# Two FFN weights loaded in 32-row pieces, and w3 transposed by VectorE in place of TensorE

## The chip, the cores and the metric

The kernel runs on one core of a Trainium2 chip. The metric is the device time of one execution in microseconds (us): before the change the median of three runs is 872.85 us, from 872.33 to 872.88. The core has five engines with a queue each: TensorE (PE; its weight loads are listed as PEld), VectorE (DVE), ScalarE (ACT), GpSimd (POOL) and SyncE (SP). Here SP only issues transfers between HBM and SBUF; some transfers are issued by ScalarE.

## The reference

Two blocks in a row. The first is a retention layer over 8 batches, 8 heads, 576 positions and a head size of 64; its result is laid out as 4608 tokens of 512 features. The second is a multiplicative feed-forward network on these tokens:

```python
    scores = scale * np.matmul(q, k.transpose(0, 1, 3, 2))
    ret = scores * Dmat[None, :, :, :]          # Dmat: gamma ** (i - j) for i >= j, else 0
    attn_out = np.matmul(ret, v).astype(np.float32)
    x = np.ascontiguousarray(attn_out.transpose(0, 2, 1, 3)).reshape(B * S, H * D)   # 4608 x 512
    a = x @ w1                                  # 512 x 1024
    b = x @ w2                                  # 512 x 1024
    h = a * b @ w3                              # 1024 x 1024
    return (h @ w_out).astype(np.float32)       # 1024 x 512
```

The four weights arrive as 64-bit floats, q, k and v as 32-bit floats. The output is 32-bit.

## The kernel before

**Algebra.** `(a * b) @ w3 @ w_out` is computed as `(a * b) @ (w3 @ w_out)`. The product w3o = w3 @ w_out (1024 x 512) is made once, on the chip, in what is called the w3 stage below. The products x @ w1, x @ w2 (the function `up`, L476 to L521) and (a * b) @ w3o (`down`, L583 to L638) use Strassen-like schemes with seven block products and sums of blocks on VectorE, ScalarE and GpSimd.

**Weights.** TensorE and VectorE work here on 32-bit floats, so each weight is converted on the chip. A weight is cut into blocks of 128 partitions by 512 numbers (the list `blocks`, L309 to L315): 16 blocks of w1 and w2, then 8 of w_out (one row tile of 128 rows each), then 16 of w3 (row tile `ft` of 128 rows, two halves of 512 columns). SP loads a block as pairs of 32-bit words into one of five `raw` buffers (`load_block`, L319), 512 KB a block; w3 and w_out blocks are one transfer each (L337). `begin_block` (L353) and `end_block` (L378) convert it: on VectorE L362 and L366 take out exponent and top mantissa, L369 adds the low word; on ScalarE L372 and L373 bring the exponent into place; on VectorE L383 adds the sign and L392 multiplies. That is five VectorE operations and two ScalarE operations for a block. The conversion is a generator (`conversion`, L401): it begins a block before it ends the one before it, and the rest of the kernel advances it by single steps (`convert`, L422, or up to a given block, `convert_up_to`, L428), which places its instructions between others in the engines' queues. When a block is ended, the block five further on is loaded into its buffer.

**The w3 stage.** TensorE contracts over partitions, so w3 @ w_out needs w3 with its columns on the partitions. `w3_tr` (L433) turns a row tile of w3 by eight TensorE transposes of 128x128 into two PSUM banks, which ScalarE copies to a tile `w3T` (L440). `w3_mm` (L443) multiplies its eight 128x128 pieces with the eight tiles of w_out, in two halves of four, into one bank `ps`, and ScalarE copies the result to `w3o` (L451). `w3` and `w3T` have two buffers each.

**Order.** Each engine works through its queue in the order in which the program emits it. The order around the stage is written by hand in the loop at L730: while products of `up` are left (`todo`), an `up` is emitted with steps of the conversion between its sums. Then, for each row tile, come the first half of the products of the tile before, the transposes of this tile, the second half of the products, and ten steps of conversion. A gate in `end_block` (L387) holds the conversion of w3 to two row tiles ahead of the transposes.

**After the stage.** `w3_sums` (L526) makes four sums of blocks of w3o on VectorE (L536); they are emitted one by one between the sums of the next `up` (`aside`). Then comes the first `down`, whose own sums are L565, L569 and L571. The attention inputs for the next two batches are loaded (L109) into SBUF space that the conversion's buffers had held, and scaled by GpSimd (L212). From 320 us on, k and q tiles are loaded in pieces of 32 rows (`load_blocks`, L168, issued at L179) and transposed by VectorE in 32x32 blocks (`front_blocks`, L198).

Of the kernel before, what the change touches and what calls it, by code (L numbers as in the profile page):

```python
# [8 lines left out]
F32 = mybir.dt.float32  # L9
I32 = mybir.dt.int32  # L10
U32 = mybir.dt.uint32
ALU = mybir.AluOpType
PSUM = bass.MemoryType.PSUM

# [22 lines left out]
def kernel(  # L39
# [13 lines left out]
    nc = tc.nc  # L53
    moe_w1, moe_w2, moe_w3, moe_w_out = (
        w.bitcast(I32).rearrange("r (c t) -> r c t", t=2) for w in (moe_w1, moe_w2, moe_w3, moe_w_out))
    B, H, S, D = q.shape
    DM = H * D
    DF = moe_w3.shape[0]
    CV = 512
    P = 128  # L60
    NP = H // 2
    NB2 = B // 2


    NC = (S + P - 1) // P
    short = S - (NC - 1) * P
    sizes = [short] + [P] * (NC - 1)
    starts = [0] + [short + c * P for c in range(NC - 1)]
    G = NB2 * NC
    NB = 3  # L70
    TB = S // NB
    NT = 2 * TB // P
    KD = DM // P
    KF = DF // P
# [13 lines left out]
    pools = {}  # L88
# [6 lines left out]
    open_attention(att_part)  # L95
    acc = ctx.enter_context(tc.tile_pool(name="acc", bufs=7, space=PSUM))
    st_ps = ctx.enter_context(tc.tile_pool(name="st_ps", bufs=1, space=PSUM))

    ctx.enter_context(tc.manual_schedule())

    live = {}
# [14 lines left out]
    ident = const.tile([P, P], F32, tag="ident", name="ident")  # L116
# [10 lines left out]
    gq = const.tile([P, NC, H], F32, tag="gq", name="gq")  # L127
    gqs = const.tile([P, NP, S // 32], F32, tag="gqs", name="gqs")
    dq = ffn.tile([P, 4, 2, TB], F32, tag="c", name="dq", bufs=1).rearrange("p a b s -> p (a b s)")[:H, :S]
# [6 lines left out]
    for c in (0, slice(1, NC)):  # L136
        n = short if c == 0 else P
# [16 lines left out]
    def strassen_weights(fp):  # L154
# [7 lines left out]
        tt("S4", "A12", "S2", ALU.subtract)  # L162
        live["S", fp] = True
        yield

    BL = 32

    def load_blocks(g, nm):  # L168

        i, c = divmod(g, NC)  # L170
        n = sizes[c] // BL
        t = pools["ld"].tile([P, 2 * NP, P // BL, BL], F32, tag="ld_q", name="bl_" + nm)
        src = {"k": k, "q": q}[nm][2 * i:2 * i + 2].rearrange("b (p a) s d -> a (b p) s d", a=2)
        for a in range(2):
            for f in range(D // BL):
                part = (a * (D // BL) + f) * BL
                for m in range(n):
                    s0 = starts[c] + m * BL
                    nc.sync.dma_start(t[part:part + BL, :, m, :],  # L179
                                      src[a, :, s0:s0 + BL, f * BL:(f + 1) * BL].rearrange("m r x -> r m x"))  # L180
        live["bl_" + nm, g] = t

    def scale_blocks(g):
# [3 lines left out]
        for b in range(2):  # L187
            part = t[:, b * NP:(b + 1) * NP, :n, :]
            nc.gpsimd.tensor_tensor(
                out=part, in0=part, in1=gqs[:, :, n0:n0 + n].unsqueeze(3).to_broadcast([P, NP, n, BL]),  # L190
                op=ALU.mult)

    def front_blocks(g):
        c = g % NC
        n = sizes[c] // BL
        for nm in "kq":
            dst = pools["fr"].tile([P, 2, NP, P], F32, tag=nm + "T", name=nm + "T", bufs=1 if nm == "k" else 2)
            nc.vector.transpose(  # L198
# [16 lines left out]
    def front(g, names="kq"):  # L215
        c = g % NC
        sz = sizes[c]
        for nm in names:
            src = live[nm, g]
            dst = pools["fr"].tile([P, 2, NP, P], F32, tag=nm + "T", name=nm + "T",  # L220
                                   bufs=1 if nm == "k" and g >= NC else 2)
# [87 lines left out]
    blocks = []  # L309
# [2 lines left out]
            for r in range(2):  # L312
                blocks.append((("w12", fp, j, r), w))
    blocks += [(("wo", g), moe_w_out) for g in range(KF)]
    blocks += [(("w3", ft, g0), moe_w3) for ft in range(KF) for g0 in range(0, DF, CV)]  # L315
    at = {key: n for n, (key, _) in enumerate(blocks)}
    loaded, begun, converted, turned = [0], [0], [0], [0]

    def load_block():  # L319
        n = loaded[0]  # L320
        if n == len(blocks):
            return
        key, w = blocks[n]
        t = raw.tile([P, CV, 2], I32, tag="raw", name="raw", bufs=5)
        if key[0] == "w12":
            _, fp, _, r = key
            src = w[2 * r * P:2 * (r + 1) * P, fp * QC:(fp + 1) * QC, :]
            t2 = t.rearrange("p (c n) t -> p c n t", c=2)
            if r == 0:
                nc.sync.dma_start(t2, src.rearrange("(c p) n t -> p c n t", p=P))  # L330
            else:
                for half in range(2):
                    nc.sync.dma_start(t2[heads[half]],
                                      src.rearrange("(c a d) n t -> a d c n t", a=2, d=D)[1 - half])
        else:
            r, c0 = (key[1], 0) if key[0] == "wo" else key[1:]
            nc.sync.dma_start(t, w[r * P:(r + 1) * P, c0:c0 + CV, :])  # L337
        live["raw", n] = t
        loaded[0] += 1

    def converted_to(n):
        key, _ = blocks[n]
        if key[0] == "w12":
            _, fp, j, r = key
            return wA[fp // 2][:, j, 2 * r:2 * r + 2, fp % 2 * QC:fp % 2 * QC + QC]
        if key[0] == "wo":
            return live["wo"][:, key[1], :]
        _, ft, g0 = key
        if ("w3", ft) not in live:
            live["w3", ft] = pools["wst"].tile([P, DF], F32, tag="w3", name="w3")  # L350
        return live["w3", ft][:, g0:g0 + CV]

    def begin_block():  # L353
        n = begun[0]
# [23 lines left out]
    def end_block():  # L378
        n = converted[0]
        hi = live["raw", n][:, :, 1]  # L380
        e, m = live["em", n]
        vec = nc.vector
        vec.scalar_tensor_tensor(e, in0=hi, scalar=-(1 << 31), in1=e,  # L383
                                 op0=ALU.bitwise_and, op1=ALU.bitwise_or)
        yield
        key = blocks[n][0]
        while not (key[0] == "w12" or "wo" in live and (key[0] == "wo" or key[1] < turned[0] + 2)):  # L387
            yield "wait"
        out, m, e = converted_to(n), m.bitcast(F32), e.bitcast(F32)
        if key[0] == "w12":  # L390
            m, e = (x.rearrange("p (c n) -> p c n", c=2) for x in (m, e))
        vec.scalar_tensor_tensor(out, in0=m, scalar=2.0 ** -20, in1=e, op0=ALU.mult, op1=ALU.mult)  # L392
        converted[0] += 1

        if n >= 4:
            load_block()
        if key[0] == "w12" and key[1] > 0 and key[2:] == (1, 1):
            yield from strassen_weights(key[1])
        yield
# [22 lines left out]
    def convert(n):  # L422

        for _ in range(n):
            if go_on() is not None:
                return

    def convert_up_to(n):  # L428
        while converted[0] < n:
            assert go_on() is None  # L430


    def w3_tr(ft):  # L433
        t = pools["wst"].tile([P, KF, P], F32, tag="w3T", name="w3T")
        for i in range(0, KF, NP):
            tp = acc.tile([P, NP, P], F32, tag="acc", name="tp")
            for n in range(NP):
                nc.tensor.transpose(tp[:, n, :], live["w3", ft][:, (i + n) * P:(i + n + 1) * P],  # L438
                                    ident)
            nc.scalar.copy(t[:, i:i + NP, :], tp)  # L440
        live["w3T", ft] = t

    def w3_mm(ft, part):  # L443
        if part == 0:
            live["w3ps"] = acc.tile([P, DM], F32, tag="acc", name="ps")
        ps = live["w3ps"]
        for g in range(part * NP, part * NP + NP):
            nc.tensor.matmul(ps, live["w3T", ft][:, g, :], live["wo"][:, g, :],  # L448
                             start=(g == 0), stop=(g == KF - 1))
        if part == 1:  # L450
            nc.scalar.copy(live["w3o"][:, ft, :], ps)  # L451

    every = [(i, n) for i in range(NB2) for n in range(NB)]

# [190 lines left out]


    load_block()
    load(0, "v")
    load_block()
    load(1, "kq")  # L650
    load_block()
# [65 lines left out]
    for a in range(2):  # L717
        for f in range(D // BL):
            part = (a * (D // BL) + f) * BL
# [6 lines left out]
    live["wo"] = pools["wst"].tile([P, KF, DM], F32, tag="wo", name="wo", bufs=1)  # L726
    live["w3o"] = w3op.tile([P, KF, DM], F32, tag="w3o", name="w3o")
    todo = [(0, 1, 2), (0, 0, 3), (0, 1, 3)] + [(0, 2, fp) for fp in range(NQ - 1)]
    multiplied = 0
    while multiplied < KF:  # L730
        if todo:
            first = converted[0] < 4 * NQ
            up(*todo.pop(0), conv=2 if first else 1)
            convert(0 if first else 3)
        ft = multiplied
        begun_ft = ft < turned[0]
        if begun_ft:
            w3_mm(ft, 0)
        if turned[0] < KF and (not todo or converted[0] > at["w3", turned[0], DF - CV]):
            convert_up_to(at["w3", turned[0], DF - CV] + 1)  # L740
            w3_tr(turned[0])
            turned[0] += 1
        if begun_ft:
            w3_mm(ft, 1)
            multiplied += 1
        if not todo:
            convert(10)
    w3_part.close()


# [15 lines left out]
    todo = [(down, (0, 0), (0, 1)), (down, (1, 0), (1, 1)), (down, (0, 2), (1, 2))]  # L766
# [38 lines left out]
    for g in range(NC, G):  # L805
        c = g % NC
        n = -(-len(todo) // (NC - c))
# [78 lines left out]
```

## Time and profile before

| What | Value |
|---|---|
| median of three runs | 872.85 us |
| profiled execution: its own time | 872.62 us |
| profiled execution: span, first to last instruction | 870.7 us |
| mean granted TensorE clock | 0.998 of full speed |
| TensorE busy | 851.9 us, 98% of the span |
| VectorE busy | 458.3 us, 53% |
| ScalarE busy | 194.7 us, 22% |
| GpSimd busy | 111.8 us, 13% |
| w3 stage on TensorE: 64 products of 128x512 (128 passes, L448) | 56.4 us busy |
| w3 stage on TensorE: 64 transposes (L438) | 8.5 us busy |
| blocks of w3 and w_out (L337), issue to landing, median | 3.6 us |

The profile is one execution, recorded by the hardware. Times are in microseconds, means of one instruction in nanoseconds. "L438" is a line of the kernel. A group of instructions is given as line, engine, operation, the tile written, an arrow, and the tiles read, with its shape. The chain that ended last is followed back from the last instruction to what released each step, so its shares tell on whose time the end depends. In a timeline a line gives start, length, engine, line, operation and count, and in square brackets how long the engine had been idle and what ended that. A TensorE product of 32-bit floats stands as two passes. Matmuls overlap, and their ends are modelled, so rows of busy matmuls add up to a little more than the time they cover; the distance from start to start is the better measure.

### The profile page before, as it was taken

The page shows a single profiled execution, that of the slowest core. Times are in us where ns is not written, and L with a number is a line of the kernel's source. Part 1 is how long each engine was busy: PE and PEld are TensorE (multiplying, and loading weights), DVE is VectorE, ACT ScalarE, POOL GpSimd, SP SyncE. Part 2 cuts the span into 40 slices and gives each one's busy share as a digit, 9 for nine tenths or more (in the row PEclk, how much of TensorE's full clock was granted, in tenths as well). Part 3 has the DMA queues.
Part 4 walks back from the last instruction along what each step waited for, and adds up shares of the span by engine and source line. Part 5 has one row for each costly group of instructions (what it writes and reads, how often), then busy time and mean ns, then how long its engine had stood idle before and what let it go on. Part 6 is the DMA issues. An engine that isn't in the chain of part 4 may idle for free.

```text
span 870.7 us, 15305 instructions
## 1 busy us (share of the span) xinstructions
PE 851.9 (98%) x6373; PEld 779.0 (89%) x6373; DVE 458.3 (53%) x781; ACT 194.7 (22%) x390; POOL 111.8 (13%) x91
## 2 busy tenths in 40 slices
PE   5899999999999999999999999999999999999998
PEld 5899999645888999999999999999999999999996
DVE  4799998973543344643544544534543434334343
ACT  3676333553022221101111101111101100001000
POOL 3000020002001323201212030230300101000000
PEclk9999999999999999999999999999999999999999
DMA  9993443437035444515242335061300000000001
GB/s 194 218 223 107 98 99 104 139 120 108 1 77 118 114 63 82 95 28 93 49 84 44 55 68 96 27 104 34 59 25 25 2 25 1 25 24 1 25 1 49
DMA packets 187332, 63.20 MB, mean 73 GB/s; under 512 B 175480, under 2 KB 175480, under 8 KB 187264
## 3 DMA queue, kind: packets, MB, share of 16 engines
q1 hardware_dynamic: 154624, 54.07, 29.2%
q10 hardware_dynamic: 32640, 8.16, 4.9%
q8 instruction: 50, 0.82, 0.4%
q14 instruction: 18, 0.15, 0.1%
HBM read 52.76 MB, written 9.44 MB: 71 GB/s over the span
## 4 chain that ended last, share of the span: by engine, by line
PE 88%; DVE 3%; issue 1%; DMA 1%; ACT 1%; DVEq 0%; ACTq 0%; SPq 0%
PE up L493 46%; PE po L599 25%; PE ps L448 6%; PE sc L241 4%; PE xps L298 3%; PE xps L291 2%; PE tp L226 1%; PE st L263 1%; DVE c L498 1%; PE tp L438 1%; DVE e L383 0%; DMA raw<-in_moe_w_dram 0%; ACT e L372 0%; DVE ab L519 0%; DVE w L392 0%
## 5 line engine op out<-in xcount | busy, mean ns | idle before, releaser
L498 DVE TENSOR_TENSOR c<-up,c 128x384 f32<-128x384 f32 x240 | 133.2, 555 | 198.0 <-PE up L493 193.2
L493 PE MATMUL up<-xT,wA 128*128 128x192 f32 x1152 | 213.5, 329 | 1.0 <-ACT xT L303 1.0
L493 PEld LDWEIGHTS up<-xT,wA 128*128 128x128 f32 x1152 | 191.9, 191 | 3.6 <-ACT xT L303 1.2
L493 PE MATMUL up<-T,wS 128*128 128x192 f32 x768 | 141.1, 327 | 2.1 <-DVE T L467 2.1
L493 PEld LDWEIGHTS up<-T,wS 128*128 128x128 f32 x768 | 127.8, 191 | 2.4 <-issue 2.4
L599 PE MATMUL po<-w3o,ab 128*128 128x256 f32 x456 | 104.2, 381 | 0.3 <-ACT ot L621 0.3
L599 PEld LDWEIGHTS po<-w3o,ab 128*128 128x128 f32 x456 | 86.0, 190 | 12.1 <-ACT ot L621 0.7
L603 DVE TENSOR_TENSOR ot<-po,ot 128x256 f32<-128x256 f32 x90 | 38.1, 424 | 72.3 <-PE po L599 70.6
L513 ACT COPY c<-up 128x384 f32<-128x384 f32 x48 | 22.9, 477 | 226.3 <-PE up L493 222.0
L493 PE MATMUL up<-xT,wS 128*128 128x192 f32 x384 | 70.6, 327 | 0.6 <-DVE c L498 0.5
L493 PE MATMUL up<-T,wA 128*128 128x192 f32 x384 | 70.3, 326 | 0.0
L244 DVE TENSOR_TENSOR pm<-sc,mask 128x512 f32<-128x512 f32 (+1 forms) x80 | 45.5, 628 | 46.7 <-PE sc L241 46.5
L599 PE MATMUL po<-wB,forms 128*128 128x256 f32 x288 | 65.1, 379 | 0.0
L493 PEld LDWEIGHTS up<-xT,wS 128*128 128x128 f32 x384 | 63.6, 190 | 1.5 <-DVE c L498 1.5
L493 PEld LDWEIGHTS up<-T,wA 128*128 128x128 f32 x384 | 63.7, 190 | 0.0
L599 PEld LDWEIGHTS po<-wB,forms 128*128 128x128 f32 x288 | 54.8, 190 | 7.3
L212 POOL TENSOR_TENSOR ld_v<-ld_v,gk 128x1024 f32<-128x1024 f32 (+1 forms) x17 | 32.3, 1900 | 213.6 <-DMA ld_v<-in_v_dram 186.3
L448 PE MATMUL ps<-wo,w3T 128*128 128x512 f32 x128 | 56.4, 593 | 0.2 <-ACT w3T L440 0.2
L506 ACT COPY c<-up 128x384 f32<-128x384 f32 x48 | 22.8, 476 | 117.4 <-PE up L493 68.4
L467 POOL TENSOR_TENSOR T<-xT,T 128x384 f32<-128x384 f32 x20 | 20.9, 1043 | 217.1 <-PE up L493 215.4
L519 DVE TENSOR_TENSOR ab<-c 128x768 f32<-128x768 f32 x48 | 46.6, 972 | 3.8
L448 PEld LDWEIGHTS ps<-wo,w3T 128*128 128x128 f32 x128 | 23.7, 190 | 27.2 <-issue 26.7
(75 smaller groups left out, 817.8 us busy)
## 6 DMA issues: line engine op xcount, KB each, us to landing
raw<-in_moe_w_dram SPq DMA_DIRECT2D x24, 512.0 KB, 3.7
out_dram<-ot SPq DMA_DIRECT2D x24, 256.0 KB, 2.0
bl_q<-in_q_dram SPq DMA_DIRECT2D x136, 32.0 KB, 2.1
bl_k<-in_k_dram SPq DMA_DIRECT2D x136, 32.0 KB, 2.2
raw<-in_moe_w_dram SPq DMA_DIRECT2D x16, 256.0 KB, 6.1
ld_k<-in_k_dram SPq DMA_DIRECT2D x8, 512.0 KB, 7.1
ld_q<-in_q_dram SPq DMA_DIRECT2D x8, 512.0 KB, 8.2
ld_v<-in_v_dram SPq DMA_DIRECT2D x8, 512.0 KB, 7.4
```

The lines of the kernel that those rows point to most:

```text
L212: nc.gpsimd.tensor_tensor(out=t, in0=t, in1=gam[:sz, c].unsqueeze(1).unsqueeze(3).to_broadcast([sz, 2, H, D]), op=ALU.mult)
L241: nc.tensor.matmul(sc[j][:sz, p, :sz], kT[hs, b, p, :sz], qT[hs, b, p, :sz], start=True, stop=True)
L244: nc.vector.tensor_mul(pm[:sz, b, j, :, :sz], sc[j][:sz, :, :sz], mask[:sz, :sz].unsqueeze(1).to_broadcast([sz, NP, sz]))
L298: nc.tensor.matmul(banks[r][heads[half], b, n, :sz], vs[:sz, b * H + 2 * p + j, :], pm[:sz, b, j, p, :sz], start=(c == 0 and m == 0), stop ...
L448: nc.tensor.matmul(ps, live["w3T", ft][:, g, :], live["wo"][:, g, :], start=(g == 0), stop=(g == KF - 1))
L493: nc.tensor.matmul(ps[:, w, :], a[:, w, r, :], b[:, r, :], start=(new and w == r == 0), stop=(w == r == 1), skip_group_check=True)
L498: nc.vector.tensor_add(c[:, to], ps, c[:, sb])
L506: nc.scalar.copy(c[:, 0], p1)
L513: nc.scalar.copy(c[:, 0], p1)
L519: nc.vector.tensor_mul(ab[:, 4 * fp:4 * fp + 4, :], c[:, :, 0, :], c[:, :, 1, :])
L599: nc.tensor.matmul(ps[nm], a[A][:, f, :], live["W"][B][:, f, :], start=(f == 0 and not on), stop=(f == NP - 1), skip_group_check=True)
L603: nc.vector.tensor_add(ot[:, to[0], to[1]], ps[nm], ot[:, sb[0], sb[1]])
```

## The change

Four things change together.

- **w_out's loads.** Row tile `i` no longer holds rows 128 i to 128 i + 127. It holds, for four groups `a` of 32 partitions, rows 256 a + 32 i to 256 a + 32 i + 31, and is loaded by four transfers of 32 rows.
- **w3's loads.** A block (row tile `ft`, half `h`) is loaded by four transfers into 32 partitions each. Group `a` of 32 partitions takes columns from the quarter `a` (256 columns) of w3; the four sub-blocks `j` of 32 rows of the tile stand beside one another in the free dimension, in pieces of 128 numbers (1 KB).
- **The transposes.** When the second half of a row tile is converted, one VectorE transpose of 32x32 blocks (128 x 1024) writes `w3T`. Because of the new places of rows and columns, its partitions then match those of w_out's tiles. `w3_tr`, its 64 TensorE transposes and its 16 ScalarE copies are gone. `w3` has one buffer, `w3T` three.
- **The order.** `w3_mm` makes all eight products of a row tile at once. The gate lets the conversion run three row tiles ahead of the products, and the loop takes eleven steps of conversion per row tile, the eleventh being the transpose.

The conversion itself keeps its operations; the last one of a w3 block writes four runs of 128 numbers.

```diff
@@ -58,6 +60,8 @@
+    BL = 32
+    QP = P // BL
...
@@ -312,9 +314,9 @@
             for r in range(2):
                 blocks.append((("w12", fp, j, r), w))
     blocks += [(("wo", g), moe_w_out) for g in range(KF)]
-    blocks += [(("w3", ft, g0), moe_w3) for ft in range(KF) for g0 in range(0, DF, CV)]
+    blocks += [(("w3", ft, h), moe_w3) for ft in range(KF) for h in range(DF // CV)]
     at = {key: n for n, (key, _) in enumerate(blocks)}
-    loaded, begun, converted, turned = [0], [0], [0], [0]
+    loaded, begun, converted, multiplied = [0], [0], [0], [0]
 
     def load_block():
         n = loaded[0]
@@ -332,9 +334,15 @@
                 for half in range(2):
                     nc.sync.dma_start(t2[heads[half]],
                                       src.rearrange("(c a d) n t -> a d c n t", a=2, d=D)[1 - half])
+        elif key[0] == "wo":
+            src = w.rearrange("(a i x) n t -> i a x n t", i=KF, x=BL)[key[1]]
+            for a in range(QP):
+                nc.sync.dma_start(t[a * BL:(a + 1) * BL], src[a])
         else:
-            r, c0 = (key[1], 0) if key[0] == "wo" else key[1:]
-            nc.sync.dma_start(t, w[r * P:(r + 1) * P, c0:c0 + CV, :])
+            _, ft, h = key
+            src = w[ft * P:(ft + 1) * P].rearrange("(j r) (a h f) t -> h a r j f t", r=BL, a=QP, h=DF // CV)
+            for a in range(QP):
+                nc.sync.dma_start(t[a * BL:(a + 1) * BL].rearrange("p (j f) t -> p j f t", j=P // BL), src[h, a])
         live["raw", n] = t
         loaded[0] += 1
 
@@ -345,10 +353,10 @@
             return wA[fp // 2][:, j, 2 * r:2 * r + 2, fp % 2 * QC:fp % 2 * QC + QC]
         if key[0] == "wo":
             return live["wo"][:, key[1], :]
-        _, ft, g0 = key
-        if ("w3", ft) not in live:
-            live["w3", ft] = pools["wst"].tile([P, DF], F32, tag="w3", name="w3")
-        return live["w3", ft][:, g0:g0 + CV]
+        _, ft, h = key
+        if h == 0:
+            live["w3"] = pools["wst"].tile([P, P // BL, DF // CV, CV // QP], F32, tag="w3", name="w3", bufs=1)
+        return live["w3"][:, :, h, :]
 
     def begin_block():
         n = begun[0]
@@ -384,12 +392,20 @@
                                  op0=ALU.bitwise_and, op1=ALU.bitwise_or)
         yield
         key = blocks[n][0]
-        while not (key[0] == "w12" or "wo" in live and (key[0] == "wo" or key[1] < turned[0] + 2)):
+        while not (key[0] == "w12" or "wo" in live and (key[0] == "wo" or key[1] < multiplied[0] + 3)):
             yield "wait"
         out, m, e = converted_to(n), m.bitcast(F32), e.bitcast(F32)
         if key[0] == "w12":
             m, e = (x.rearrange("p (c n) -> p c n", c=2) for x in (m, e))
+        if key[0] == "w3":
+            m, e = (x.rearrange("p (c n) -> p c n", c=P // BL) for x in (m, e))
         vec.scalar_tensor_tensor(out, in0=m, scalar=2.0 ** -20, in1=e, op0=ALU.mult, op1=ALU.mult)
+        if key[0] == "w3" and key[2] == DF // CV - 1:
+            yield
+            t = pools["wst"].tile([P, KF, P], F32, tag="w3T", name="w3T", bufs=3)
+            vec.transpose(t.rearrange("p i (j r) -> p j i r", r=BL),
+                          live["w3"].rearrange("p j h f -> p (j h f)"))
+            live["w3T", key[1]] = t
         converted[0] += 1
 
         if n >= 4:
@@ -430,25 +446,13 @@
             assert go_on() is None
 
 
-    def w3_tr(ft):
-        t = pools["wst"].tile([P, KF, P], F32, tag="w3T", name="w3T")
-        for i in range(0, KF, NP):
-            tp = acc.tile([P, NP, P], F32, tag="acc", name="tp")
-            for n in range(NP):
-                nc.tensor.transpose(tp[:, n, :], live["w3", ft][:, (i + n) * P:(i + n + 1) * P],
-                                    ident)
-            nc.scalar.copy(t[:, i:i + NP, :], tp)
-        live["w3T", ft] = t
-
-    def w3_mm(ft, part):
-        if part == 0:
-            live["w3ps"] = acc.tile([P, DM], F32, tag="acc", name="ps")
-        ps = live["w3ps"]
-        for g in range(part * NP, part * NP + NP):
+    def w3_mm(ft):
+        ps = acc.tile([P, DM], F32, tag="acc", name="ps")
+        for g in range(KF):
             nc.tensor.matmul(ps, live["w3T", ft][:, g, :], live["wo"][:, g, :],
                              start=(g == 0), stop=(g == KF - 1))
-        if part == 1:
-            nc.scalar.copy(live["w3o"][:, ft, :], ps)
+        nc.scalar.copy(live["w3o"][:, ft, :], ps)
+        multiplied[0] += 1
 
     every = [(i, n) for i in range(NB2) for n in range(NB)]
 
@@ -726,25 +730,19 @@
     live["wo"] = pools["wst"].tile([P, KF, DM], F32, tag="wo", name="wo", bufs=1)
     live["w3o"] = w3op.tile([P, KF, DM], F32, tag="w3o", name="w3o")
     todo = [(0, 1, 2), (0, 0, 3), (0, 1, 3)] + [(0, 2, fp) for fp in range(NQ - 1)]
-    multiplied = 0
-    while multiplied < KF:
+    while multiplied[0] < KF:
+        ft = multiplied[0]
+        done = at["w3", ft, DF // CV - 1] + 1
+        ready = converted[0] >= done
         if todo:
             first = converted[0] < 4 * NQ
             up(*todo.pop(0), conv=2 if first else 1)
             convert(0 if first else 3)
-        ft = multiplied
-        begun_ft = ft < turned[0]
-        if begun_ft:
-            w3_mm(ft, 0)
-        if turned[0] < KF and (not todo or converted[0] > at["w3", turned[0], DF - CV]):
-            convert_up_to(at["w3", turned[0], DF - CV] + 1)
-            w3_tr(turned[0])
-            turned[0] += 1
-        if begun_ft:
-            w3_mm(ft, 1)
-            multiplied += 1
+        if ready or not todo:
+            convert_up_to(done)
+            w3_mm(ft)
         if not todo:
-            convert(10)
+            convert(11)
     w3_part.close()
```

More of the change, by code (lines that the diff above doesn't have):

```diff
@@ L164, in strassen_weights @@
         yield
-    BL = 32
     def load_blocks(g, nm):
```

## The prediction

> **What bounds the kernel now.** I read the page's busy times first, then the chain that ended last, then the timelines of the stage that the diff touches. TensorE has work for 98% of the span and carries 88% of the chain, so time is won only where TensorE issues less or waits less.
>
> ```profile
> PE 851.9 (98%) x6373; PEld 779.0 (89%) x6373; DVE 458.3 (53%) x781; ACT 194.7 (22%) x390; POOL 111.8 (13%) x91
> PE 88%; DVE 3%; issue 1%; DMA 1%; ACT 1%; DVEq 0%; ACTq 0%; SPq 0%
> ```
>
> VectorE's 53% is an average. In the w3 stage, by the windows, it is busy 33.8 us of the 40 from 160 to 200. TensorE's timeline there (start, length, engine, line, operation; in brackets the idle time before it and what ended it):
>
> ```profile
> 158.79 1.04 PE L438 MATMUL tp<-ident,w 128*128 128x128 f32 x8
> 160.07 3.70 PE L448 MATMUL ps<-wo,w3T 128*128 128x512 f32 x8 [0.24 <-ACT w3T L440]
> 165.35 0.63 PE L438 MATMUL tp<-ident,w 128*128 128x128 f32 x4 [1.14 <-DVE w L392]
> 165.81 7.03 PE L448 MATMUL ps<-wo,w3T 128*128 128x512 f32 x16
> 172.68 1.04 PE L438 MATMUL tp<-ident,w 128*128 128x128 f32 x8
> 173.56 7.03 PE L448 MATMUL ps<-wo,w3T 128*128 128x512 f32 x16
> 222.57 1.46 PE L493 MATMUL up<-xT,wA 128*128 128x192 f32 x8
> ```
>
> The stage lasts from 158.79 to 222.57, 63.8 us. Row blocks repeat every 7.74 us: 0.87 of transposes, 6.87 of products. Eight of each are 7.0 and 55.0; the other 1.8 us are start and waits. VectorE and ScalarE, same stage:
>
> ```profile
> 184.35 0.69 DVE L369 SCALAR_TENSOR_TENSOR m<-raw,m 128x512 f32<-128x512 uint32 x1
> 186.92 0.69 DVE L383 SCALAR_TENSOR_TENSOR e<-raw,e 128x512 int32<-128x512 int32 x1 [1.88 <-ACT e L373]
> 187.72 0.69 DVE L392 SCALAR_TENSOR_TENSOR w<-m,e 128x512 f32<-128x512 f32 x1
> 184.93 0.58 ACT L451 COPY w3o<-ps 128x512 f32<-128x512 f32 x1 [2.79 <-PE ps L448]
> ```
>
> ScalarE takes w3o's copy in order, so the exponent operations behind it wait for the products, and VectorE waits for them. This costs nothing today.
>
> **What the Trainium skill says.** "VectorE: DVE Perf Modes", section The three transpose paths: VectorE transposes 32x32 blocks only; hence the loads by 32 rows. "SBUF — State Buffer", section Door 1: a transfer into 32 partitions reaches 8 of 16 ports, 189 GB/s at 1 MiB; no row of before tests that with long packets. Same page, Who interferes with whom: a VectorE operation with two SBUF inputs and a GpSimd operation that reads SBUF exclude each other. The trace agrees: L624 took 1.40 us while GpSimd ran, and 0.69 at 237.05 without it.
>
> ```profile
> 253.13 1.90 POOL L212 TENSOR_TENSOR ld_q<-ld_q,gq 128x1024 f32<-128x1024 f32 x1 [33.58 <-DMA ld_q<-in_q_dram]
> 254.18 1.40 DVE L624 TENSOR_TENSOR ab<-ab,forms 128x512 f32<-128x512 f32 x1 [6.07 <-PE po L599]
> ```
>
> **The change part by part.** TensorE loses 64 transposes (8 x 0.87 = 7.0 us) and the waits on their copies. The floor is 55.0 us, so at most 8.8 us can be won. ScalarE loses 16 copies of 0.59, which were not on the path.
>
> VectorE gains eight transposes of 128x1024. The same operation, fp32 and of that size, is in the trace:
>
> ```profile
> L198 DVE STREAM_TRANSPOSE kT<-bl_k x9: 705/1239/1245, 346.9 to 647.8; 128x1024 f32<-128x1024 f32 x8, 128x512 f32<-128x512 f32 x1
> L198 DVE STREAM_TRANSPOSE qT<-bl_q x9: 670/1202/1205, 348.0 to 648.9; 128x1024 f32<-128x1024 f32 x8, 128x512 f32<-128x512 f32 x1
> ```
>
> From start to start they cost 1.16 us. The new ones write runs of 32 elements apart, which L198 does only in its 128x512 form, at no visible price. I take 1.16; bounds 1.0 and 1.5. Per row block VectorE needs two blocks of conversion, each 0.34 + 0.45 + 0.61 to begin (1.40) and 0.72 + 0.73 to end (1.45), and the transpose: 5.70 + 1.16 = 6.86. That equals TensorE's 6.87, so VectorE's waits, free before, become the stage's.
>
> Follow them. By the order in the built program only the first transpose falls before the stage, between the third and fourth additions of the last up (done about 158.5, in time for 158.8, and after the addition that TensorE's reuse of p5 waits for). It pushes ab and what follows later: before, L392 of that block started 161.65; I put the third block's end at 163.2. Then begin, end, transpose: the second w3T is ready at 167.2, while the first product ends at 165.7: TensorE waits 1.6 us. In program order w3o's copy stands before the next four exponent operations, so the first of these is usable 2.19 us after the end of products two row blocks earlier (0.2 to the copy, 0.48, then twice 0.75, from the rows at 177), the second 3.53 after. From 167.2: begin to 168.6; ScalarE allows L383 at 165.7 + 2.19 = 167.9, no wait; end 170.0, begin 171.4, end 172.9, transpose 174.1. From there: begin to 175.5; the products that began at 167.3 end at 174.2, so L383 may start at 176.4 and waits 0.9; end 177.8, begin 179.2, end 180.7, transpose 181.8. Stepping on so, 0.12 us from transpose to product, gives w3T ready at 167.2, 174.1, 181.8, 188.7, 196.5, 203.4, 209.7; intervals alternate 6.9 and 7.8, because every second time L383 waits about 0.9 us. The last products end at 217.2 instead of 222.57: a gain of **5.35 us**. A transpose of 1.0 gives 216.7, of 1.5 gives 218.6; four landing waits instead of one at each begin, at up to 0.1 us, give 217.8.
>
> Transfers: w3 goes from 16 to 64, w_out from 8 to 32. Issue took 0.33 us for a whole-tile transfer, 0.31 at the fastest and 0.95 as a mean (15.21 us for 16 bl_k) for 32-row ones; I take 0.6, so 2.4 us a block. Moving 512 KB through 8 ports at 189 GB/s is 2.8 us, an estimate from the page. VectorE takes a block every 3.5 us or more, and five buffers stand ahead. The last w3 block, served serially at 2.8 us from 156.2 (when the sixth can start), lands 15 us early. The built program lets each issue wait for the eighth transfer before it, now two blocks back instead of eight; a block took 3.6 us to land, and two are converted in 7, so this holds nothing up. w_out's extra 24 issues (about 8 us of SP) are spread over 40 us; the sixteen gqs loads move about 1 us and the sixth w_out block, needed at 126.4, lands near 118. Cost nothing; uncovered it would be the DMA rival below.
>
> What moves: the next attention loads follow the last conversions on SP. Before, k went at 203.13, released by L383; the corresponding L383 now starts at 203.5 + 2.19 and ends about 206.4, so these loads and the GpSimd scalings move 3.3 us later, while TensorE comes 5.35 earlier. They keep some 12 us to their use at 244. But the scalings of 215.50 and 217.65 now fall at 218.8 to 222.9, on VectorE's four w3 sums (L536, two SBUF inputs), which start near 220.6 and run without a gap:
>
> ```profile
> 225.92 1.21 DVE L536 TENSOR_TENSOR w3o<-w3o 128x1024 f32<-128x1024 f32 x1
> 232.35 0.68 DVE L565 TENSOR_TENSOR ab<-ab 128x512 f32<-128x512 f32 x1
> ```
>
> L565 ends at 233.03 and down's second product reads it at 231.67 + 1.73 = 233.40: 0.35 us to spare. One scaling in the way delays the sums about 1.5 us, so TensorE waits 1.1; bounds 0 and 2.5. Nothing later on SP or GpSimd moves against TensorE.
>
> Sum: the profiled run is 872.62 (span 870.7 and 1.9 around it), less 5.35, plus 1.1: 868.4; the median of the runs lies 0.23 higher, so **868.6**.
>
> **Rivals.**
> - *No collision with GpSimd*: if the scalings miss the sums, 867.5. For it: the two windows only touch. Chance 0.2.
> - *TensorE floor*: w3T always early, all 8.8 won, 864.1. Against it: 6.86 against 6.87, and the copy in ScalarE's order. Chance 0.03.
> - *Dear transposes*: at twice L198's price (2.32) the stage ends at 222.3, nothing won, 872.6 to 873.7. Only the scattered writes speak for it. With 2.0: 220.6, about 872. Chance 0.1.
> - *Slower: DMA becomes the bound.* The last block can land at 156.2 + 11p + 2 for p us a block; 5.5 us of conversion and transpose and 6.9 of products follow. Up to p = 4.2 nothing changes, at 4.7 the gain is gone, at 5 the end is 225.6 and the time 876. For it: 16 bl_k issues took 0.95 each, four of which are 3.8. Against it: those carried 256 packets of 128 bytes, these 128 of 1 KB. Chance 0.1.
>
> **How the numbers follow.** The likeliest case has 0.57 and its own range 867.0 to 870.5 (collision 0 to 2.5, transpose 1.0 to 1.5). The range reaches down to include the no-collision case with a cheap transpose, 866.6, and up into dearer transposes, 871.1; the floor, half of the dear transposes and the DMA case stay out, about 0.2. A change under 0.2% (1.75 us) is what a measurement can't tell from none. Faster: 0.57 + 0.2 + 0.03 = 0.80; dear transposes are split between same (0.08) and slower (0.02), and DMA adds 0.1 to slower.
>
> **What would show it.** Right: no matmul between the products, L198-like transposes of about 1.2 us, TensorE waiting on w3T about 1.6 us before the second row block and 0.9 before every other later one, L383 waiting on ScalarE, products ending near 217. Wrong: waits of L362 on DMA, transposes far from 1.2 us, or a longer wait in down than 2.5 us.

## The result and the profile after

| | before | changed | ratio, 95% interval |
|---|---|---|---|
| median of four runs each | 872.87 us | 869.33 us | 0.9958 (0.994 to 0.9975) |
| profiled execution, its own time | 872.62 us | 869.44 us | |
| profiled execution, span | 870.7 us | 867.5 us | |
| w3 stage on TensorE, first of its matmuls to the next up | 63.78 us | 58.79 us | |
| from there to the first product of the second down (the up and the down after the stage, and the attention's products that follow them) | 26.22 us | 27.23 us | |

The changed kernel is 3.5 us faster by the medians; 4.25 were forecast, 868.6 us. The stage gave 5.0 us, and the up and the down after it took 1.0 back. From the second down to the end both profiles take 621.9 us. Lines of the changed kernel are numbered a little higher: L362, L383 and L392 of the conversion are now L370, L391 and L402, the products L448 are L452, the copy to w3o L451 is L454, the sums L536 are L540, and L406 is the new transpose.

The page of the changed kernel, busy times and chain:

```profile
PE 845.7 (97%) x6309; PEld 771.2 (89%) x6309; DVE 468.0 (54%) x789; ACT 185.9 (21%) x374; POOL 115.3 (13%) x91
PE 86%; DVE 7%; DMA 3%; issue 2%; ACT 1%; SPq 1%; POOL 0%; DVEq 0%; ACTq 0%; POOLq 0%
```

TensorE lost its 64 transposes and 6.2 us of busy time. VectorE's share of the chain went from 3% to 7%, but this is no measure of the change: in the second profiles shown below it is 6% before and 5% after. That the stage now hangs on VectorE is read from TensorE's timeline there:

```profile
159.60 7.03 PE L452 MATMUL ps<-wo,w3T 128*128 128x512 f32 x16
167.94 13.97 PE L452 MATMUL ps<-wo,w3T 128*128 128x512 f32 x32 [1.31 <-DVE w3T L406]
182.75 14.10 PE L452 MATMUL ps<-wo,w3T 128*128 128x512 f32 x32 [0.84 <-DVE w3T L406]
197.58 20.97 PE L452 MATMUL ps<-wo,w3T 128*128 128x512 f32 x48 [0.74 <-DVE w3T L406]
218.39 1.46 PE L497 MATMUL up<-xT,wA 128*128 128x192 f32 x8
```

The row blocks follow one another except at three places: before the second, the fourth and the sixth, TensorE waits for VectorE's transpose. Three of VectorE's rows and three of ScalarE's, at the fourth row block, show why:

```profile
175.31 0.69 DVE L377 SCALAR_TENSOR_TENSOR m<-raw,m 128x512 f32<-128x512 uint32 x1
177.07 0.69 DVE L391 SCALAR_TENSOR_TENSOR e<-raw,e 128x512 int32<-128x512 int32 x1 [1.07 <-ACT e L381]
181.45 1.25 DVE L406 STREAM_TRANSPOSE w3T<-w 128x1024 f32<-128x1024 f32 x1
```

```profile
175.08 0.59 ACT L454 COPY w3o<-ps 128x512 f32<-128x512 f32 x1 [5.09 <-PE ps L452]
175.56 0.73 ACT L380 ACTIVATE e<-e,lim 128x512 int32<-128x512 int32 x1
176.32 0.72 ACT L381 ACTIVATE e<-e,lim 128x512 int32<-128x512 int32 x1
```

VectorE stands idle for 1.07 us before L391, because ScalarE held the exponent operations back behind the copy of a finished product. In the kernel before such waits came to 6.5 us and cost nothing; here they come to 2.9 us in three waits (1.07, 0.94 and 0.86), and the first two of them reach TensorE, before the fourth and the sixth row block. The rows of the two new operations (shortest, median and longest in ns, first and last start):

```profile
L406 DVE STREAM_TRANSPOSE w3T<-w x8: 1239/1245/1245, 158.1 to 209.6; 128x1024 f32<-128x1024 f32 x8
L345 SPq DMA_DIRECT2D raw<-in_moe_w_dram x64: 311/430/437, 126.5 to 193.9; - x64
```

The transposes cost what the kernel's other transposes cost. An issue of a 32-row transfer took 0.43 us and its landing 3.0 us at the median. A whole block landed about 4.4 us after its first issue, against 3.6 before. Between 80 and 215 us VectorE waited for no transfer.

### The profile page after: what moved, and what is told of

It reads as the page before. It is cut to its first block, busy times and chain, and to the rows that moved or that the text cites. A ratio compares the mean times of both kernels' runs of the same rounds, so it can differ in the third digit from the quotient of the medians.

```text
span 867.5 us, 15264 instructions
## 1 busy us (share of the span) xinstructions
PE 845.7 (97%) x6309; PEld 771.2 (89%) x6309; DVE 468.0 (54%) x789; ACT 185.9 (21%) x374; POOL 115.3 (13%) x91
## 4 chain that ended last, share of the span: by engine, by line
PE 86%; DVE 7%; DMA 3%; issue 2%; ACT 1%; SPq 1%; POOL 0%; DVEq 0%; ACTq 0%; POOLq 0%
PE up L497 46%; PE po L603 24%; PE ps L452 4%; PE sc L243 4%; PE xps L300 3%; PE xps L293 2%; PE tp L228 2%; PE st L265 1%; DVE c L502 1%; DMA ld_q<-in_q_dram 1%; DVE e L391 1%; DMA ld_k<-in_k_dram 1%; DVE w L402 1%; DVE pm L246 1%; DVE m L377 1%
## 5 line engine op out<-in xcount | busy, mean ns | idle before, releaser
L452 PE MATMUL ps<-wo,w3T 128*128 128x512 f32 x128 | 56.1, 596 | 2.9 <-DVE w3T L406 2.9
L452 PEld LDWEIGHTS ps<-wo,w3T 128*128 128x128 f32 x128 | 23.8, 190 | 34.4 <-issue 30.6
```

## The experiments

There were eight runs: the two kernels once more, unaltered, and six altered kernels. The table measures the stage from its first matmul, so that what happened before it does not count; the last column is the sum of the two before it. "Up and down after it" ends where the second down begins. The kernel before had a median of 873.30 us beside the first four kernels with a ratio, and of 873.51 beside the last three.

| kernel | median | ratio to before (95%) | stage | up and down after it | both |
|---|---|---|---|---|---|
| before, profile again | 873.85, one run | | 63.77 | 26.23 | 90.00 |
| changed, again | 869.45 | 0.9956 (0.9942 to 0.9971) | 58.78 | 27.33 | 86.11 |
| copy to w3o later on ScalarE | 866.82 | 0.9928 (0.9915 to 0.9942) | 56.55 | 27.10 | 83.65 |
| second v tile loaded later | 868.68 | 0.9953 (0.9939 to 0.9967) | 58.79 | 26.22 | 85.01 |
| both | 865.55 | 0.9915 (0.990 to 0.993) | 56.56 | 26.22 | 82.78 |
| transposes twice | 877.13 | 1.0053 (1.0035 to 1.0071) | 65.81 | 26.94 | 92.75 |
| w3 by 16 rows | 869.41 | 0.996 (0.9946 to 0.9975) | 58.80 | 27.23 | 86.03 |
| before, with split transfers | 872.77 | 0.9994 (0.9985 to 1.0002) | 63.78 | 26.22 | 90.00 |

### The stage began late in the first profile

In the profile of the changed kernel the stage began at 159.60, in that of the kernel before at 158.79, although nothing that the change touches had run by 80 us. VectorE's timeline, beside GpSimd's, shows this at 46 us:

```profile
45.85 2.49 POOL L214 TENSOR_TENSOR ld_q<-ld_q,gq 128x1024 f32<-128x1024 f32 x1 [21.41 <-PE tp L228]
46.61 2.27 DVE L402 SCALAR_TENSOR_TENSOR wA<-m,e 128x512 f32<-128x512 f32 x1
```

A multiplication of the conversion, 0.69 us elsewhere, took 2.27 us; a GpSimd scaling had begun just ahead of it. Both kernels were run again unaltered.

> The changed kernel once more, unaltered. Theory: the 0.80 us by which the stage began late in the first profile of it (products from 159.60 instead of 158.79) come from chance in how a GpSimd scaling and a VectorE conversion met at 46 us, before anything that the change touches. Then the stage begins in this profile between 158.7 and 159.7, not tied to 159.6, and the median lies within 0.5 us of 869.3. Rival: the change itself causes it, through the w_out transfers; then the stage begins at 159.6 again.

> The kernel before once more, unaltered, for a second profile. If the meeting at 46 us is chance, its stage begins anywhere between 158.5 and 159.7, with a VectorE operation of over 2 us near 46 where it begins late.

The changed kernel's stage began at 158.35 this time. The kernel before now showed the same meeting, and its stage began at 160.02:

```profile
46.66 2.09 POOL L212 TENSOR_TENSOR ld_q<-ld_q,gq 128x1024 f32<-128x1024 f32 x1 [21.79 <-DMA ld_q<-in_q_dram]
47.03 2.27 DVE L392 SCALAR_TENSOR_TENSOR wA<-m,e 128x512 f32<-128x512 f32 x1
```

So the lag is chance, of one execution and not of a kernel: each kernel has an early and a late profile, 1.2 us apart. Both starts lay about 0.3 us outside of what was expected, one below 158.7, the other above 159.7. The medians of the two kernels stayed near where they were: 872.87, then 873.30 and 873.51 before the change, 869.33, then 869.45 after it.

The meeting at 46 us is not the whole of it. The same eight products of an up took 2.45 us in the first profile of the changed kernel and 1.54 in the second, some ten microseconds earlier:

```profile
35.58 2.45 PE L497 MATMUL up<-xT,wA 128*128 128x192 f32 x8
35.69 1.54 PE L497 MATMUL up<-xT,wA 128*128 128x192 f32 x8
```

From 30 to 40 us the mean granted TensorE clock was 0.83 in the first of them (0.50 from 35 to 37) and 1.00 in the second. In the first, TensorE was 0.64 us ahead of the second at 33.5 us and 0.80 behind it at 43. Six of the ten profiles of this study have 0.83 there, both of the kernel before among them; in them the stage began between 158.79 and 160.02, and all four meetings with a VectorE operation of over 2 us are among these six. In the four with 1.00, TensorE was ready for the stage between 158.04 and 159.07. The clock alone does not settle it: the two profiles of the kernel before both have 0.83, and the later one has the meeting. Nor does the meeting: the profile with 16-row transfers, below, has the low clock and no meeting, and its stage began at 159.48. How much of the lag is due to each stays open.

### ScalarE's order, and the scaling beside the sums

```diff
@@ w3_mm
-        nc.scalar.copy(live["w3o"][:, ft, :], ps)
         multiplied[0] += 1
+        return lambda: nc.scalar.copy(live["w3o"][:, ft, :], ps)
@@ the loop of the stage
+        copy = None
         if ready or not todo:
             convert_up_to(done)
-            w3_mm(ft)
+            copy = w3_mm(ft)
         if not todo:
             convert(11)
+        if copy:
+            copy()
```

> The copy of the products to w3o is put on ScalarE's queue behind the four exponent operations that followed it. Theory (VectorE's row block of 6.83 us equals TensorE's 6.87, and the rest of TensorE's waits come from ScalarE's order): L391 no longer waits for ScalarE (2.9 us before), TensorE waits only before the second row block (about 1.3 us), products end about 2.4 us earlier than in the changed kernel, and the next loads are released some 3 us earlier: 2.3 to 3.3 us faster than it, 866 to 867. Rival (VectorE's own work bounds the stage, its waits being covered): within 0.5 us of the changed kernel.

Products run without a gap from the second row block on; the median is 2.6 us below the changed kernel's:

```profile
159.79 7.03 PE L452 MATMUL ps<-wo,w3T 128*128 128x512 f32 x16
168.12 48.38 PE L452 MATMUL ps<-wo,w3T 128*128 128x512 f32 x112 [1.31 <-DVE w3T L406]
```

L391's waits for ScalarE are gone from the list, the stage is 2.2 us shorter (56.55), and only the wait before the second row block is left. The three waits on TensorE, 1.31, 0.84 and 0.74, thus have two causes. The first is VectorE's own work: in the changed kernel VectorE ran without a wait from the first transpose at 158.05 to the end of the second at 167.79, and with the transposes doubled, below, this wait grew to 2.67. The other two, gone here, were ScalarE's order. The next loads were released 3.0 us earlier (204.45 instead of 207.46), but the scaling met the sums all the same, now the first of them (2.33 us), and up and down stayed 0.9 us longer than before the change.

That meeting was the object of the next kernel. Timeline of the changed kernel, GpSimd and VectorE:

```profile
221.74 1.22 DVE L540 TENSOR_TENSOR w3o<-w3o 128x1024 f32<-128x1024 f32 x1
221.97 2.74 POOL L214 TENSOR_TENSOR ld_v<-ld_v,gk 128x1024 f32<-128x1024 f32 x1 [0.23 <-DMA ld_v<-in_v_dram]
223.34 2.46 DVE L540 TENSOR_TENSOR wB<-w3o 128x1024 f32<-128x1024 f32 x1
```

The scaling takes 2.74 us instead of 1.90 and the second sum 2.46 instead of 1.21. The starts suggest that each waits for the other in turn: the scaling for the first sum, the second sum for the scaling. TensorE's down then waits for the sum behind them:

```profile
227.72 1.89 PE L603 MATMUL po<-w3o,ab 128*128 128x256 f32 x8
230.12 3.72 PE L603 MATMUL po<-w3o,ab 128*128 128x256 f32 x16 [0.51 <-DVE ab L569]
```

```diff
-    for g in (NC, NC + 1):
-        load(g, "kqv")
+    load(NC, "kqv")
+    load(NC + 1, "kq")
     keep_stores.clear()
     store()
+    load(NC + 1, "v")
```

> Only the load of the second v tile after the stage is issued later, behind the first down's stores, so that its scaling on GpSimd no longer runs beside VectorE's four sums of w3o. Theory (that meeting costs TensorE 1.0 us between 218 and 246: 0.23 in up and 0.78 in down): no sum above 1.25 us, no wait in down for L569, 1.0 us faster than the changed kernel. Rival (down was late for another reason): no difference, or a loss, if v is then late for the state product near 259.

The sum is back at its own length, and down runs through. The rows of VectorE and TensorE in this kernel:

```profile
222.35 1.21 DVE L540 TENSOR_TENSOR wB<-w3o 128x1024 f32<-128x1024 f32 x1
226.50 5.34 PE L603 MATMUL po<-w3o,ab 128*128 128x256 f32 x24
```

Up and down after the stage take 26.22 us, exactly as before the change, 1.0 less than in the changed kernel. By the medians the difference to the changed kernel is 0.8 us, and the two intervals overlap, so it is the trace that shows it, not the time alone. The v tile was scaled by 247.4 and used at 256.9.

> Both edits together. Theory: the stage's 2.4 us and down's 1.0 us are separate, so 3.3 us faster than the changed kernel, about 866. Rival: the earlier end of the stage moves other loads or scalings onto VectorE's sums, and less than 2.5 us is left.

The two add up: 58.79 + 27.23 = 86.02 became 56.56 + 26.22 = 82.78, 3.24 us. The median, 865.55 us, is 3.9 below the changed kernel's in the same comparison and 0.85% below the kernel before. This is the fastest version of the study.

### How level VectorE and TensorE are

```diff
-            vec.transpose(t.rearrange("p i (j r) -> p j i r", r=BL),
-                          live["w3"].rearrange("p j h f -> p (j h f)"))
+            for _ in range(2):
+                vec.transpose(t.rearrange("p i (j r) -> p j i r", r=BL),
+                              live["w3"].rearrange("p j h f -> p (j h f)"))
```

> The changed kernel with every VectorE transpose of w3 done twice, into the same place. Theory (VectorE and TensorE are level in the stage): each row block takes VectorE 8.0 us instead of 6.83, less what its waits for ScalarE give back, so products end about 4.5 to 6 us later and the whole gain is gone: 873.5 to 876. Rival (slack on VectorE): under 2 us more than the changed kernel.

It is 7.7 us slower than the changed kernel, more than expected, and slower than the kernel before. TensorE's waits there, in total, times and longest, and the first two of them:

```profile
PE ps L453 <- DVE w3T L407: 9.1, 6, 2.7
160.03 7.11 PE L453 MATMUL ps<-wo,w3T 128*128 128x512 f32 x16 [0.96 <-DVE w3T L407]
169.81 15.46 PE L453 MATMUL ps<-wo,w3T 128*128 128x512 f32 x32 [2.67 <-DVE w3T L407]
```

A pair takes VectorE 2.45 us from start to start, 1.28 more than one transpose, so there are 10.2 us more of VectorE work. In the traces 7.7 us of it reach TensorE: the first pair makes the stage itself begin 0.96 us late, which the expectation had left out, and the last column of the table is 6.7 us longer than in the first profile of the changed kernel. Up to 1.3 us of this may be the clock's: the granted clock was 0.83 from 165 to 175 us in this profile, two row blocks took 15.46 us there instead of 13.97, and VectorE waited for ScalarE behind them once, for 1.28 us. The two runs with a mean clock of 0.998 took 876.29 and 876.73, the two with less (0.996 and 0.994) 877.52 and 880.13. Either way most of the added work reaches the end, far more than the 2 us of the rival: VectorE has little slack in the stage.

### The transfers

```diff
             for a in range(QP):
-                nc.sync.dma_start(t[a * BL:(a + 1) * BL].rearrange("p (j f) t -> p j f t", j=P // BL), src[h, a])
+                for u in range(2):
+                    half = slice(u * BL // 2, (u + 1) * BL // 2)
+                    nc.sync.dma_start(
+                        t[a * BL + u * BL // 2:a * BL + (u + 1) * BL // 2].rearrange("p (j f) t -> p j f t", j=P // BL),
+                        src[h, a][half])
```

> The changed kernel with w3 loaded by 16 rows, eight transfers a block instead of four. Theory (transfers lie hidden, with up to 4.2 us a block to spare): at 0.43 us an issue a block takes SP 3.4 us instead of 1.7, under what the stage uses a block in, so the time stays within 0.5 us of the changed kernel. Rival (the small transfers are near the bound): waits of L370 on DMA appear and it is over 2 us slower.

With twice as many transfers (128 issues at 0.42 us) the median is 869.41 against 869.45, and the stage is the same to 0.01 us. VectorE still waited for no transfer between 120 and 215 us. There was less to spare than the median shows, though. During the stage SP did little but issue these transfers:

```profile
159.68 39.47 SPq L347 DMA_DIRECT2D raw<-in_moe_w_dram  x73
```

From start to start an issue took 0.47 us, so a block took 3.75 us or more and not 3.4, while the stage took a block every 3.7. The last block landed 3.3 us before VectorE began it, against 7.4 in the changed kernel.

In the kernel before, the one line that loads a block of w_out or w3 was split by rows:

```diff
-            nc.sync.dma_start(t, w[r * P:(r + 1) * P, c0:c0 + CV, :])
+            for a in range(P // BL):
+                nc.sync.dma_start(t[a * BL:(a + 1) * BL], w[r * P + a * BL:r * P + (a + 1) * BL, c0:c0 + CV, :])
```

> The kernel before, with nothing but its w_out and w3 blocks split into four transfers of 32 rows each; layout, order and TensorE's transposes stay. Theory: the transfers cost nothing, within 0.5 us of the kernel before. Rival: they cost part of what the change gave away (its gain was 0.7 us under the forecast): 0.7 us slower or more.

The ratio is 0.9994, its interval includes 1, and the median lies 0.7 us under the kernel before, 0.2 beyond what was expected, on the faster side. By its profile the stage takes 63.78 us and the rest 26.22, as in the kernel before. So the shorter transfers cost nothing in this layout; in the new one the 16-row run speaks for the same.

## Why the prediction was right

The direction, the size and the range held: 869.33 against 868.6, within 866.6 to 871.1. Step by step:

- **The floor of 55.0 us and the 7.0 us of transposes.** Right. With ScalarE's order mended the stage still takes 56.55 us: the floor and the wait before the second row block.
- **A transpose at 1.16 us from start to start, scattered writes free.** Right: 1.245 us each and 1.17 from start to start. The rival of dear transposes falls. One reading that this leant on was not exact: the short form of L198 writes runs of 64 numbers, not of 32 (64 positions of each row of 128), so it was no test of the new writes.
- **VectorE level with TensorE, 6.86 against 6.87.** Right: a row block without a wait took VectorE 6.83 us, and the doubled transposes show that most of what is added there reaches the end.
- **When w3T is ready.** Forecast for the stage's start at 158.8: 167.2, 174.1, 181.8, 188.7, 196.5, 203.4, 209.7. Measured, less the 0.80 by which this execution was late: 167.0, 173.8, 181.9, 188.8, 196.7, 203.7, 210.1. The alternation of long and short intervals, from ScalarE's queue, is there.
- **The stage, 58.4 us.** It measured 58.8. From start to start, less 6.87 us of products, TensorE lost 1.47, 1.00 and 0.97 us before the second, fourth and sixth row blocks, where 1.6, 0.86 and 0.96 were forecast. The other 0.4 us were lost before the third, fifth, seventh and eighth row blocks, 0.07 to 0.12 each, which the forecast had let follow without a loss. These are the terms that were sized too small.
- **Transfers hidden.** Right, with 0.43 us an issue instead of the 0.6 taken. The DMA rival falls: even 16-row transfers did not make VectorE wait, though they left little room. The last block did not land 15 us early but 7.4: it is loaded when a buffer comes free, and the forecast had served the blocks without a pause.
- **The scaling on the w3 sums.** Right in place and cause, with one sum delayed by 1.25 us where 1.5 were forecast; the price was 1.0 us against 1.1 forecast, 0.23 in up and 0.78 in down. Loading v later takes away the whole of it. The rival without a collision did not come about in any profile of the changed kernel.
- **The median.** The stage and the collision give 86.02 instead of the 85.75 forecast, 0.27 of the 0.7 us missed. The rest is smaller than the chance ahead of the stage, which puts two profiles of one kernel 1.2 us apart; the second comparison gave a difference of 3.85 us by the medians where the first gave 3.54. How near the medians came is thus in part luck; the stage and the collision, read apart, are not.

What the prediction did not see is the chance before the stage, in the granted clock and in the meeting at 46 us, which both kernels show.

## What to carry to other kernels

Moving work from the bound engine to one with idle time paid here only up to the point where the two were level in that stage, whatever the average over the span; then waits that were covered before, here a copy in front of unrelated operations on a third engine's queue, became the price, and reordering that queue was worth another 2.2 us. When a stage ends earlier, look at what starts after it: loads tied to another engine's progress move by a different amount, and work that never overlapped may meet. Compare profiles from the start of the stage that changed, and read the granted clock ahead of it, so that chance there is not taken for the change. Read a share of the chain from two profiles of a kernel before calling its rise an effect.

## What the runs showed of the hardware that was not expected

- When a GpSimd scaling met two VectorE sums in a row, both engines lost: the scaling took 2.74 us instead of 1.90 and the second sum 2.46 instead of 1.21. In the kernel with the later copy the scaling began first and kept its 1.90, and the first sum took 2.33. In the repeated profiles of one and the same kernel a scaling and a multiplication of the conversion near 46 us met (2.27 us instead of 0.69) or missed each other.
- The granted TensorE clock fell to half at a different time in different profiles: it was 0.50 from 35 to 37 us in the first profile of the changed kernel, 1.00 there in its second, and 0.50 from 170 to 172 us with the doubled transposes. A mean of 0.83 over ten microseconds is about 3.4 us at half, an estimate from these figures. Of 19 runs of the kernel before, the seven with a mean clock of 0.999 or more have a median of 872.33 us, the twelve below it 873.76.
- The 32x32 transposes that write runs of 32 numbers, 128 numbers apart, cost the same 1.245 us as those of L198 that write their output in one piece (1.239).
